# A new instruction order for a fused attention and token-MLP kernel, with vector work, row statistics and small loads moved between engines

## The chip, the cores and the metric

The kernel runs on one core of a Trainium2 chip. The metric is device time of one execution in microseconds (us), on the slowest core, which here is the only one. A profiled span, from the first to the last instruction, is about 1.8 us shorter than the time of the same run. Times of whole runs and spans of traces are therefore never mixed below: where stages are added up, the sum is a span.

The engines are PE (matmul), DVE (vector), ACT (activation functions), POOL (a second, general engine for elementwise work) and SP (which mostly issues DMAs). In the profile, PEld is PE's loading of weights, and a q after an engine's name is its instruction queue. Each executes its own list of instructions in order.

## The reference

Two branches share the input x (2048 tokens x 448) and are mixed by a gate per token. Cut to what matters:

```python
g = sigmoid((x * gate_w).sum(-1, keepdims=True))
# A: attention in 4 segments of 512 tokens, 16 heads of 28, plus a linear memory
phi = lambda t: where(t > 0, t + 1.0, exp(t))
for s in range(4):
    p = softmax(qs @ ks.T * scale + mask);  a_dot = p @ vs
    pq = phi(qs);  a_mem = (pq @ M) / (pq @ z + 1e-6)
    outs.append(sigmoid(beta) * a_mem + (1 - sigmoid(beta)) * a_dot)
    pk = phi(ks);  M = M + pk.T @ vs;  z = z + pk.sum(tokens)
a = concat(outs) @ wo
# B: LayerNorm over features, then an MLP over TOKENS
h = (x - mean) / sqrt(var + 1e-5)
u = gelu(einsum('bsd,sf->bdf', h, w1) + b1)          # w1 2048 x 1792
b = (einsum('bdf,fs->bds', u, w2) + b2).transpose(0, 2, 1)
return g * a + (1 - g) * b
```

## The kernel before

The kernel is a list of 1020 small operations in one string, PLAN. An item `name.args@engine+slots` names an operation, the engine that does it (P = PE, A = ACT, D = DVE, G = POOL, S = SP) and its buffers. A scheduler walks the string once, appends each operation to its engine's list and works out the semaphore waits from what each reads and writes. So the order in the string is the order of each engine, and changing a letter moves work between engines without touching the data flow.

```python
PLAN = """
warm@P ldwk.0@A dve0@D id@G ldx.0@S ldx.1@S ldwq.0@A setup@G ldwk.1@S acttab@A ldwq.1@S ldsm@S xw.0@D bn.0@D trx.0.3@P
...
ek.1.2@A pqm.1.1@G1 bn.8@D ldr.1@S1 pqe.1.0@A0 u.0.0@P0 u.1.0@P3 bn.12@D sc.0.2@P lnc.2@G u.1.1@P pqe.1.1@A1 ev.6@D
...                                                                                     (77 more lines)
```

phi is written as min(max(t, 0) + 1, exp(t)): a clamp (`pkm`, `pqm`), an exponential on ACT (`pke`, `pqe`) and a minimum on DVE (`pkn`, `pqn`). Five of the 12 clamps are on DVE and seven on POOL.

```python
def pmax(eng, dst, Rd, T, RT, hp, s):                      # pkm, pqm: the clamp, 128 x 1024
    op(eng, lambda e: e.tensor_scalar(dst..., two(T, hp, s), 0.0, 1.0, op0=ALU.max, op1=ALU.add), ...)
def pmin(dst, Rd, i):                                      # pkn, pqn
    op("DVE", lambda e: e.tensor_tensor(dst, dst, et[:, i, :], op=ALU.min), ...)
```

The LN has statistics on DVE (`bn`), a combination per four tiles on POOL (`lnc`), and an apply per tile (`lna`), eight on DVE and eight on POOL:

```python
def bn(eng, u, t):
    op("DVE", lambda e: e.bn_stats(st6[:, t, :], xtile(t)[:, 0, :]), ...)
    op("DVE", lambda e: e.bn_aggr(mv[:, t, :], st6[:, t, :]), ...)
def lnc(eng, u, g):     # 4 POOL operations on 128 x 4
    ... vpe = var + eps;  rstd = vpe ** -0.5;  vpe = -mean;  nmr = vpe * rstd
def lna(eng, u, t):
    op(eng, lambda e: e.tensor_scalar(x_t, x_t, rstd[:, t:t+1], nmr[:, t:t+1], op0=ALU.mult, op1=ALU.add), ...)
```

At the start DVE fills padded buffers with zeros, SP issues five small loads (gate weights, two biases, beta), and two copies of 128 x 128 (`xw`) widen the first x tiles. Part of the first PE transposes (`trx`) read what these copies write, and everything else on PE, apart from the warm-up matmuls (`NWARM` is their number), comes after the transposes:

```python
def dve0(eng, u):
    ...
    op("DVE", lambda e: e.memset(oAM[:], 0.0), writes=R_o)       # 128 x 3072 bf16
    op("DVE", lambda e: e.memset(wo_sb[:], 0.0), writes=[R_woz])
def xw(eng, u, h):
    op("DVE", lambda e: e.tensor_copy(x0[:, r, D:512], x0[:, r, 0:64]), reads=R_x[r], writes=R_xw[r])
def ldsm(eng, u): ...   # five dma_start by eng: gate_w (2), b1, b2, beta
```

The softmax here doesn't subtract the row's maximum and nothing guards it: scores larger than these inputs give would overflow.

## Time and profile before

| | before |
|---|---|
| time, median of 3 runs | 199.17 us (198.92 to 200.08) |
| span of the trace | 197.3 us |
| busy: PE / DVE / ACT / POOL | 176.7 / 143.8 / 118.5 / 84.4 us |
| share of the chain that ended last (the work followed back from the last instruction, at each step to what released it): PE / DVE / POOL | 38 / 25 / 23% |

The columns are length, then busy us of PE, PEld, DVE, ACT and POOL, the granted PE clock (1.00 is full), DMA share and GB/s.

```profile
31.00:35.00 4.00, 0.17 (x2) 0.10 (x2) 3.86 (x12) 0.70 (x2) 3.55 (x7) 1.00 1.32 208
35.40:38.80 3.40, 3.40 (x19) 1.00 (x19) 2.38 (x3) 1.88 (x1) 3.14 (x5) 0.50 0.78 160
100.20:103.60 3.40, 3.40 (x23) 1.08 (x24) 0.93 (x2) 3.33 (x3) 0.63 (x1) 0.50 0.16 40
```

The first is the 3.83 us wait of PE for the LN apply on POOL. The second comes right after it: PE is busy all of the time, but its clock is 0.50. The third, again 3.4 us at half clock, follows the second long wait (3.23 us, to 98.7). In this trace a long wait is paid for twice. And two groups of DVE in this trace (columns: line, engine, operation, output <- input, count, busy us, mean ns):

```profile
L618 DVE TENSOR_TENSOR t<-t 128x1024 bf16<-128x1024 bf16 x12 | 13.7, 1158 | 4.2 <-POOL t L609 4.1
L509 DVE COPY t<-t 128x128 bf16<-128x128 bf16 x2 | 0.3, 144 | 0.0
```

L618 is the minimum of phi. L509 are the two `xw` copies: 144 ns each, nobody would look at them.

### The profile page before, as it was taken

What the parts mean: (1) busy time and instruction counts of PE and PEld (TensorE: products, weight loads), DVE (VectorE), ACT (ScalarE), POOL (GpSimd) and SP (SyncE); (2) the same over time, 40 slices, a digit from 0 to 9 for tenths busy, and PEclk for the clock granted to TensorE, in tenths of its full rate; (3) what the DMA queues carried; (4) which work ended last, traced back from release to release, by engine and by line L of the source; (5) the groups of instructions that cost most, each with busy time, mean ns of one, the idle gap of its engine ahead of it and who ended that gap; (6) DMA issues with size and microseconds to landing.
All of it is one profiled execution on the core that took longest, in us unless ns stands there. A gap on an engine that the chain in (4) does not pass through costs nothing.

```text
span 197.3 us, 3599 instructions
## 1 busy us (share of the span) xinstructions
PE 176.7 (90%) x1464; PEld 79.9 (40%) x1471; DVE 143.8 (73%) x272; ACT 118.5 (60%) x108; POOL 84.4 (43%) x85
## 2 busy tenths in 40 slices
PE   7399993999599989989399997999999999999994
PEld 2243441234244434434235433444334444555554
DVE  5989999698718775479848938677999975397222
ACT  3338874349658956997366698598747787201100
POOL 2052299949922823779713239331523233220000
PEclk9999999699999999999969999999999999999999
DMA  6999999678587000218116064151073407166112
GB/s 163 208 233 268 240 208 236 136 185 219 137 182 205 12 0 3 53 27 221 23 26 186 5 186 145 44 151 35 31 205 106 127 27 216 53 200 190 56 33 71
DMA packets 50368, 24.92 MB, mean 126 GB/s; under 512 B 15088, under 2 KB 49968, under 8 KB 50352
## 3 DMA queue, kind: packets, MB, share of 16 engines
q1 hardware_dynamic: 49424, 24.24, 49.9%
q10 hardware_dynamic: 928, 0.46, 1.0%
q8 instruction: 11, 0.18, 0.4%
q14 instruction: 5, 0.04, 0.1%
HBM read 18.54 MB, written 1.84 MB: 103 GB/s over the span
## 4 chain that ended last, share of the span: by engine, by line
PE 38%; DVE 25%; POOL 23%; issue 6%; DMA 2%; SPq 2%; ACT 2%; another core or an unknown queue 0%; POOLq 0%; DVEq 0%
PE t L884 14%; POOL t L609 13%; PE t L831 10%; PE t L857 4%; POOL t L718 4%; PE t L736 3%; DVE t L367 3%; DVE t L618 3%; DVE t L791 3%; DMA t<-in_A_beta_dram 2%; PE t L695 2%; PE t L571 2%; POOL t L819 2%; DVE t L870 2%; SPq L357 2%
## 5 line engine op out<-in xcount | busy, mean ns | idle before, releaser
L705 ACT ACTIVATE t<-t 128x2048 bf16<-128x2048 f32 x40 | 75.1, 1877 | 30.8 <-PE t L695 28.2
L718 POOL TENSOR_SCALAR_AFFINE_SELECT t<-t 128x1024 bf16<-128x1024 bf16 (+1 forms) x40 | 38.0, 951 | 65.4 <-ACT t L705 61.0
L831 PE MATMUL t<-t 128*128 128x448 bf16 x224 | 49.8, 361 | 3.9 <-POOL t L819 3.8
L884 PE MATMUL t<-t 128*128 128x448 bf16 (+1 forms) x238 | 45.9, 342 | 0.1
L831 PEld LDWEIGHTS t<-t 128*128 128x128 bf16 x224 | 19.9, 99 | 27.5 <-issue 7.4
L884 PEld LDWEIGHTS t<-t 128*128 128x128 bf16 x238 | 22.6, 98 | 20.2 <-issue 2.3
L546 PE MATMUL t<-t 64*128 64x512 bf16 x224 | 27.5, 388 | 0.7 <-DVE t L469 0.3
L609 POOL TENSOR_SCALAR t<-t 128x1024 bf16<-128x1024 bf16 x7 | 26.5, 3795 | 1.6 <-DVE t L367 1.1
L365 ACT ACTIVATE t<-t 128x512 bf16<-128x512 f32 (+3 forms) x27 | 15.7, 599 | 12.8 <-PE t L546 6.0
L893 DVE SCALAR_TENSOR_TENSOR t<-t 128x448 bf16<-128x448 f32 (+1 forms) x17 | 10.7, 636 | 14.6 <-PE t L884 14.6
L367 DVE CAST t<-t 128x512 bf16<-128x512 f32 (+1 forms) x23 | 15.0, 654 | 8.0 <-PE t L546 6.1
L618 DVE TENSOR_TENSOR t<-t 128x1024 bf16<-128x1024 bf16 x12 | 13.7, 1158 | 4.2 <-POOL t L609 4.1
L546 PEld LDWEIGHTS t<-t 64*128 64x128 bf16 x224 | 10.4, 96 | 15.5 <-issue 3.1
L695 PE MATMUL t<-t 28*128 28x512 bf16 (+3 forms) x256 | 16.1, 304 | 0.1
L756 DVE STREAM_TRANSPOSE t<-t 128x512 f32<-128x512 f32 x16 | 11.2, 707 | 5.8 <-PE t L736 5.6
L571 PE MATMUL t<-t 64*128 64x449 bf16 x112 | 12.0, 350 | 2.8 <-DVE t L367 2.1
L857 PE MATMUL t<-t 128*128 128x448 bf16 x64 | 13.8, 354 | 0.0
L736 PE MATMUL t<-t 128*32 128x512 bf16 (+3 forms) x256 | 12.0, 312 | 1.4 <-POOL t L718 1.1
L842 DVE TENSOR_SCALAR t<-t 128x448 bf16<-128x448 f32 x10 | 6.7, 673 | 8.9 <-PE t L831 8.9
L614 ACT ACTIVATE t<-t 128x1024 bf16<-128x1024 bf16 x12 | 12.3, 1060 | 0.0
L777 DVE SCALAR_TENSOR_TENSOR t<-t 128x448 bf16<-128x448 f32 x16 | 11.9, 753 | 0.3
L796 DVE STREAM_TRANSPOSE t<-t 128x512 bf16<-128x512 bf16 x16 | 11.0, 697 | 0.1
(70 smaller groups left out, 151.9 us busy)
## 6 DMA issues: line engine op xcount, KB each, us to landing
t<-in_B_w_dram SPq DMA_DIRECT2D x7, 1024.0 KB, 6.3
t<-in_B_w_dram SPq DMA_DIRECT2D x8, 896.0 KB, 5.2
out_dram<-t SPq DMA_DIRECT2D x15, 112.0 KB, 1.7
t<-in_A_x_dram SPq DMA_DIRECT2D x3, 448.0 KB, 4.3
t<-t SPq DMA_DIRECT2D x6, 192.0 KB, 3.4
t<-in_A_wv_dram SPq DMA_DIRECT2D x2, 392.0 KB, 5.4
t<-in_A_x_dram SPq DMA_DIRECT2D x2, 224.0 KB, 3.6
t<-in_A_wo_dram SPq DMA_DIRECT2D x4, 98.0 KB
```

The source lines that it names most:

```text
L367: op(eng, lambda e: e.tensor_copy(out, in_), reads=reads, writes=writes)
L546: last = e.matmul(bank(bb)[:, 0:512], wkq[half[h], c, 128 * hg : 128 * hg + 128], xTb[half[h], b, i, :], start=(i == 0), stop=(i == 6), sk ...
L571: last = e.matmul(bank(bs[h])[:, 0 : D + 1], xTb[half[h], b, i, k0 : k0 + 128], wvx[half[h], (LC, UC)[h][i], 0 : D + 1], start=(i == 0), s ...
L609: op(eng, lambda e: e.tensor_scalar(dst.rearrange("p (g t) -> p g t", g=2), two(T, hp, s), 0.0, 1.0, op0=ALU.max, op1=ALU.add), reads=[RT[ ...
L618: op("DVE", lambda e: e.tensor_tensor(dst, dst, et[:, i, :], op=ALU.min), reads=[Rd, R_et[i]], writes=[Rd])
L695: last = e.matmul(bank(hl)[:, c0 : c0 + w], kT[r, hg, s * 512 + j * 128 : s * 512 + j * 128 + 128], qT[r, hg, s * 512 + 128 * j : s * 512 ...
L705: op("ACT", lambda e: e.activation(punit(i).rearrange("p (a q) -> p a q", a=4), ps[:, 0:4, :], ACT.Exp, scale=SCALE), reads=R_bank[0:4], w ...
L718: op("POOL", lambda e: e.affine_select(d, d, pattern=pat, compare_op=ALU.is_ge, fill=0.0, base=0, channel_multiplier=-1), reads=[R_P[i]], ...
L736: last = e.matmul(bank(b)[32 * hl : 32 * hl + 32, 128 * j : 512], vaug[:, 4 * s + j, 32 * h : 32 * h + 32], p4[:, hl, c0 : c0 + w], start= ...
L831: op("PE", lambda e: e.matmul(bank(b)[:, 0:D], w[:, st, (ft % 2) * 128 : (ft % 2) * 128 + 128], xtile(st)[:, 0, :], start=(st == 0), stop= ...
L857: last = e.matmul(bank(b)[:, 0:D], oT[:, hg, T * 128 : T * 128 + 128], wo_sb[:, hg, :], start=(hg == 0), stop=(hg == NHG - 1), skip_group_ ...
L884: op("PE", lambda e, b=b, f=f, c0=c0, n=n: e.matmul(bank(b)[:, 0:n], w[:, f, c : c + 128], uT[:, f, c0 : c0 + n], start=(f == 0), stop=(f ...
```

## The change

The intent is to take slow work off POOL, to give the row statistics to POOL instead, to free SP of small issues, and to plan the order anew with measured durations. The same 1020 operations are kept. By engine, 7 clamps, 8 LN applies and 6 products of the memory part go from POOL to DVE; some output scalings and copies go from DVE to ACT. The core of the diff, cut:

```diff
-NWARM = 8
+NWARM = 7
 PLAN = """            # all 79 lines differ; the start and one clamp, as an example
-warm@P ldwk.0@A dve0@D id@G ldx.0@S ldx.1@S ldwq.0@A setup@G ldwk.1@S acttab@A ldwq.1@S ldsm@S xw.0@D bn.0@D trx.0.3@P
+warm@P ldwk.0@A dve0@D id@G ldx.0@S ldx.1@S ldwq.0@A ldsm@G ldwk.1@S acttab@A ldwq.1@S ldwv.0@S trx.0.2@P xw.0@D
-... pqm.1.1@G1 ...
+... pqm.1.1@D1 ...
 def dve0(eng, u):
-    op("DVE", lambda e: e.memset(oAM[:], 0.0), writes=R_o)
 def setup(eng, u):
+    op("POOL", lambda e: e.memset(oAM[:], 0.0), writes=R_o)
 def bn(eng, u, t):
-    op("DVE", lambda e: e.bn_aggr(mv[:, t, :], st6[:, t, :]), ...)
 def lnc(eng, u, g):
-    ...                       # 4 POOL operations from mean and variance
+    tt2(d, me, mo, ALU.subtract, True)      # me, se, mo, so: halves' means and sums in st6
+    tt2(d, d, d, ALU.mult)
+    tt2(w, se, so, ALU.add, True)
+    ts2(w, w, 1.0 / D, 1e-5, ALU.add)
+    ts2(d, d, 0.25, 0.0, ALU.add)
+    tt2(d, d, w, ALU.add)
+    ... rstd = d ** -0.5; tt2(sd, me, mo, ALU.add); ts2(sd, sd, -0.5, ...); nmr = sd * rstd    # 10 in all
```

Line numbers shift: the clamp is L609 before and L608 after, the minimum L618 and L617, the LN apply L819 and L833, the `xw` copy L509 and L508.

## The prediction

> **What bounds the kernel now.** I read the page first, then the chain of work that ended last, the costliest groups, the table of 10 us windows, and the timelines of the engines where these pointed.
>
> ```profile
> span 197.3 us, 3599 instructions
> PE 176.7 (90%) x1464; PEld 79.9 (40%) x1471; DVE 143.8 (73%) x272; ACT 118.5 (60%) x108; POOL 84.4 (43%) x85
> ...
> PE 38%; DVE 25%; POOL 23%; issue 6%; DMA 2%; SPq 2%; ACT 2%; another core or an unknown queue 0%; POOLq 0%; DVEq 0%
> ```
>
> PE is busiest by far, yet it is only 38% of the chain that ended last. POOL, busy 43%, is 23% of that chain: 45 us in which the end waited for POOL. So this is a PE-bound kernel that is held up.
>
> ```profile
> L609 POOL TENSOR_SCALAR t<-t 128x1024 bf16<-128x1024 bf16 x7 | 26.5, 3795 | 1.6 <-DVE t L367 1.1
> L609 DVE TENSOR_SCALAR t<-t 128x1024 bf16<-128x1024 bf16 x5 | 2.9, 588 | 0.0
> L819 POOL TENSOR_SCALAR t<-t 128x448 bf16<-128x448 bf16 x8 | 5.7, 714 | 0.2
> L819 DVE TENSOR_SCALAR t<-t 128x448 bf16<-128x448 bf16 x8 | 4.2, 564 | 0.0
> L811 POOL TENSOR_TENSOR t<-t 128x4 f32<-128x4 f32 x4 | 4.4, 1108 | 0.3
> ```
>
> These groups show whose work it is. L609 is the clamp of phi, max(t,0)+1: 3795 ns on POOL against 588 ns on DVE for the same shape. L819 applies the LN, L811 is its power -0.5. The chain in order of time shows it on the path:
>
> ```profile
> 28.02 4.04 POOL t L609
> ...
> 44.10 7.61 POOL t L609 x2
> 51.73 1.10 DVE t L618
> 52.83 0.61 DVE t L367
> 53.49 1.50 PE t L571 x14
> ```
>
> Two clamps on POOL, then the DVE minimum that needs them, then a PSUM copy queued behind that minimum, then PE. An in-order DVE carries POOL's delay to PE. The wait view has the other direct case:
>
> ```profile
> PE t L831 <- POOL t L819: 3.8, 1, 3.8
> PE t L749 <- DVE t L842: 3.2, 1, 3.2
> PE t L571 <- DVE t L367: 2.1, 1, 2.1
> ```
>
> The first is PE at 31 us waiting for the LN on POOL. The second is at 95 to 98.7 us, behind three clamps and two products on POOL. The windows say when the bound changes (columns: length, then busy us of PE, PEld, DVE, ACT, POOL, clock, DMA share, GB/s):
>
> ```profile
> 30.00:40.00 10.00, 6.17 (x35) 1.89 (x37) 8.20 (x17) 3.58 (x3) 9.20 (x14) 0.83 1.00 182
> 90.00:100.00 10.00, 6.77 (x64) 3.31 (x61) 8.77 (x15) 4.58 (x6) 7.22 (x6) 1.00 0.40 107
> 140.00:150.00 10.00, 9.11 (x76) 3.93 (x76) 9.86 (x18) 5.63 (x3) 3.22 (x4) 1.00 0.40 116
> 180.00:190.00 10.00, 10.00 (x54) 5.16 (x53) 2.84 (x4) 1.45 (x2) 0.00 (x0) 1.00 0.40 118
> ```
>
> Early, POOL and DVE starve PE; around 145 DVE is full; the end is pure PE. The change can win little in the last 40 us.
>
> **What the Trainium skill says.** (1) "GPSIMD Engine Reference", section "4.1 Engine selection", calls POOL about 2x slower for two-input elementwise work and one-input work "roughly line-rate". The trace disagrees for the clamp: 3795 / 588 = 6.5x. (2) "SBUF — State Buffer", section "Who interferes with whom": copy and tensor_scalar on DVE in a 2-port mode share a port pair with POOL, and the second to issue fully blocks. The trace agrees in direction: the DVE clamp took 0.42 us at 21.75, with POOL idle, and 1.25 us at 28.49, beside the POOL clamp of 4.06 us; not blocked to its end, though. The LN apply took 0.35 us alone and 0.95 us beside POOL. So clearing POOL also shortens DVE. (3) "DMA: Bandwidth & Descriptors", section "SWDGE vs HWDGE vs iDMA": a DMA issued by POOL has its descriptors made in software, exposed to that same port lock. No run so far has one. (4) "TensorE: Matmul & The Clock Gate", section "Back-to-back issue gap": N/2.4 + 2.5 ns, 189 ns for 448 columns. The last 80 matmuls (52 of 448 columns, 28 of 224) took 12.53 us, 190 ns per 448: PE there is at its rate (the same section's 131 ns for a sustained stream at 512 columns is not seen here).
>
> **The change part by part.** The two order lists hold the same 1020 operations; engines, banks and order differ.
>
> Clamps: 7 leave POOL, -26.5 us there, and cost DVE 7 x 0.42 = 2.9 us. LN applies: 8 leave POOL, -5.7, and cost DVE 8 x 0.45 = 3.6 (between 0.35 and 0.56). Six products of the memory part (L785, 1073 ns on POOL, 628 on DVE): -6.4 and +3.8. Statistics: 16 aggregates leave DVE, 16 x 0.182 = -2.9; POOL does 10 small operations per group instead of 4, six more at about 0.27 from start to start, 4 x 6 x 0.27 = +6.5. The zero fill of the product buffer, 1.34, goes from DVE to POOL. Four output scalings, one bias copy and one weight padding go from DVE to ACT (-2.6 - 0.6 - 0.9), one PSUM copy comes (+0.6). Sums: POOL 84.4 - 26.5 - 5.7 - 6.4 + 6.5 + 1.3 = 54; DVE 143.8 + 2.9 + 3.6 + 3.8 - 2.9 - 1.3 - 2.6 - 0.6 - 0.9 + 0.6 = 146, perhaps 3 to 5 lower for the port; ACT 118.5 + 4 x 0.72 + 0.6 + 0.9 - 0.5 = 122. PE loses one warm-up matmul, nothing else.
>
> What is on the path? I cut both lists at the first score block (L695) of each of the eight score groups, P0 to P7, and summed each engine's work in every stage with durations of the trace before (start-to-start, us): token MLP matmul 0.19, Q/K pair 1.52, V pair 1.37, score block 0.33, PV 0.66, output projection 0.76, state 0.95; DVE copies 0.6, min 0.8, clamp 0.4, transpose 0.63; exp 1.8; mask 0.95. The stage's floor is its busiest engine; what the stage took above that is waiting. Stage starts are the L695 starts of the PE timeline: 16.3, 44.15, 63.0, 80.5, 99.8, 121.4, 140.1, 155.7.
>
> ```
> stage  before: took  floor     excess | after: floor  my estimate
> start         16.3   DVE 14.8   1.5   |  DVE 12.9     14.5
> P0            27.8   DVE 23.6   4.2   |  DVE 22.6     25.0
> P1            18.8   PE 16.0    2.8   |  DVE 14.8     16.6
> P2            17.5   PE 16.0    1.5   |  PE 14.4      16.0
> P3            19.3   PE 15.0    4.3   |  PE 13.1      14.8
> P4            21.6   PE 19.4    2.2   |  PE 21.4      23.3
> P5            18.7   PE 16.9    1.8   |  PE 20.1      21.8
> P6            15.6   DVE 14.0   1.6   |  PE 13.8      15.3
> P7 to end     41.6   PE 38.0    3.6   |  PE 37.3      40.9
> sum          197.2       173.7 23.5   |      170.4    188.2
> ```
>
> The three stages with POOL on the chain (P0, P1, P3) have 11.3 us of excess; the others 1.5 to 2.2 each (P7's includes a 2.5 us tail of last copy and store). I gave the changed stages the excess of the quiet ones, 1.5 to 1.9, and P0 2.4, since DVE is nearly full there. That takes 5.4 off these three and 0.3 off the others; the rest comes from floors, 173.7 - 170.4 = 3.3, because the new order spreads PE and DVE more evenly. A run took about 1.8 more than the traced span (199.0 against 197.3), so this table gives 190.0. A plan with true durations should also wait less in the quiet stages. If excess there fell from 1.7 to about 1.2, eight times 0.5 takes 4 off: 186. I choose the middle, **188.0 us**, 0.944 of before.
>
> **The rivals.** (a) **DVE takes POOL's place.** DVE keeps 146 us and is the floor of the first three stages, 50 of 188 us; the minimum and the PSUM copies queue on one in-order engine. For it: 140:150 shows 9.86 of 10 busy and PE still waiting. Against it: its sum hardly grows, and P4 to P7 leave it 15.2, 15.0, 8.4, 23.7 against PE's 21.4, 20.1, 13.8, 37.3. It would make 193 to 196. (b) **Transfers hold the front.** DMA share is 0.92 to 1.09 in the first 40 us, and the last x tile landed at 28.05. For it: bytes do not change. Against it: no compute engine waited over 0.3 us for a large load, and taking five small issues off SP (3.27 to 5.40 us, 2.1 us) moves the large ones up. If it holds, P0 loses 3 us: 191. (c) **Small loads through POOL come late.** They gate a tanh that stands on ACT before the weight padding and the first copies, and the transposed biases before V. Before, they landed at 9.7, already a 1.9 us wait of PE. If software descriptors push them to 12, the start grows by 2 us: 190. (d) **Full success:** excess under 1 us everywhere, 182.
>
> **Range and chances.** Range 182 to 194: (d) below; (a) or (b) with (c) above. Within 2% would need over 195.2, almost nothing gained though 26 us of POOL leaves the chain; only a strong (a) does that. Faster by over 2%: 0.91; within 2%: 0.07; slower: 0.02.
>
> **What would show the steps right or wrong.** Right: POOL busy near 54 and under 10% of the chain; all L609-type clamps on DVE at 0.4 to 0.6 us; PE's share of the chain well over half; stages P0, P1, P3 at about 25, 17, 15; PE's waits for LN and for the copies behind the minimum gone; DVE 141 to 147. Wrong: DVE over 35% of the chain with PE waiting for PSUM copies (a); PE or DVE waits for loads of x or W1 in the first 40 us (b); ACT or PE idle until a beta landing at about 10 us or later (c); a quiet stage (P4, P5) that takes over 2.5 us above its floor, which would mean that the new order is worse than its sums.

## The result, and the profile after

The median of four runs is **190.77 us** (190.20 to 191.28); the kernel before had 199.62 us in the same rounds (198.92 to 200.81). The ratio is 0.955, with a 95% interval of 0.949 to 0.961. Ratios here are the mean time of one kernel's fast runs over that of the other's of the same rounds, so not quite the ratio of the medians. Predicted were 188.0 us, 2.8 us (1.5%) too few, and a range of 182 to 194. The head and the chain of the page after:

```profile
span 188.6 us, 3618 instructions
PE 175.7 (93%) x1470; PEld 81.9 (43%) x1470; DVE 140.2 (74%) x271; ACT 122.2 (65%) x110; POOL 57.8 (31%) x94
...
PE 66%; DVE 19%; POOL 4%; issue 3%; ACT 2%; DMA 2%; SPq 1%; DVEq 0%
```

PE did the same work in 8.7 us less. POOL's share of the chain fell from 23% to 4%, PE's rose from 38% to 66%. The costliest groups that answer to those shown of before:

```profile
L617 DVE TENSOR_TENSOR t<-t 128x1024 bf16<-128x1024 bf16 x12 | 9.7, 805 | 0.0
L833 DVE TENSOR_SCALAR t<-t 128x448 bf16<-128x448 bf16 x16 | 8.1, 534 | 1.3 <-POOL t L829 1.2
L608 DVE TENSOR_SCALAR t<-t 128x1024 bf16<-128x1024 bf16 x12 | 5.8, 483 | 2.2 <-DMA t<-t 1.3 <-ACT t L364 0.8
L508 DVE COPY t<-t 128x128 bf16<-128x128 bf16 x2 | 3.5, 2600 | 0.0
```

All 12 clamps are on DVE at 483 ns. The minimum, which nobody touched, fell from 1158 to 805 ns, and the sum of the two branches (128 x 512) from 705 to 443 ns. But the two little copies went from 144 to 2600 ns each (they overlap: together 3.5 us). The waits of PE that are left (columns: total us, times, longest us):

```profile
PE t L517 <- DVE t L508: 2.1, 1, 2.1
...
PE t L845 <- DVE t L833: 1.3, 1, 1.3
PE t L659 <- DVE t L759: 1.1, 1, 1.1
```

The waits of 3.8 and 3.2 us are gone. The longest single one left is at the start, for those copies. Cut at the first score block of each of the eight groups, as in the prediction:

```
stage     before   predicted   after   off    floor   above floor
start      16.3      14.5      20.9   +6.4    12.9       8.0
P0         27.8      25.0      22.0   -3.0    22.6      -0.6
P1         18.8      16.6      17.9   +1.3    14.8       3.1
P2         17.5      16.0      16.1   +0.1    14.4       1.7
P3         19.3      14.8      14.0   -0.8    13.1       0.9
P4         21.6      23.3      22.3   -1.0    21.4       0.9
P5         18.7      21.8      20.6   -1.2    20.1       0.5
P6         15.6      15.3      14.2   -1.1    13.8       0.4
P7 to end  41.6      40.9      40.7   -0.2    37.3       3.4
span      197.3     188.2     188.6
```

(The stages of before add up to 197.2 and those of after to 188.7, from rounding. The floor is the prediction's, with durations of the trace before; DVE's work in P0 took less than that, so P0 lies below it.) The total of this table is nearly exact, and that is luck: the start took 6.4 us more than predicted, the rest 6.0 less. (The 188.0 us took another 2 us off what this table gives, for a better plan.) So there is something in the start to find. The trace after there (columns: start us, duration us, engine, line, operation):

```profile
3.75 0.58 POOL L356 DMA_DIRECT2D t<-in_A_beta_dram  x1
...
4.12 3.49 DVE L508 COPY t<-t 128x128 bf16<-128x128 bf16 x2
...
4.84 2.68 POOL L443 MEMSET t<- 128x3072 bf16 x1
...
7.63 2.10 PE L517 MATMUL t<-t 128*128 128x128 bf16 x18 [2.08 <-DVE t L508]
...
11.00 4.62 PE L545 MATMUL t<-t 64*128 64x512 bf16 x28 [1.27 <-DVE t L366]
```

And the first Q/K pair of before:

```profile
9.85 1.69 PE L546 MATMUL t<-t 64*128 64x512 bf16 x14
```

The copies began at 4.12, in the middle of a row of POOL instructions (DMA issues from 1.45 to 4.33, fills from 4.33 to 7.52), and ended at 7.57 and 7.61, right after the last fill. PE waited 2.08 us and then ran slowly: 28 matmuls of the first pairs took 4.62 us, against 2 x 1.69 before.

### The profile page after: what moved, and what is told of

It is laid out like the page before. It is cut to its first block, busy times and chain, and to the rows that moved or that the text cites. A ratio compares the mean times of both kernels' runs of the same rounds, so it can differ in the third digit from the quotient of the medians.

```text
span 188.6 us, 3618 instructions
## 1 busy us (share of the span) xinstructions
PE 175.7 (93%) x1470; PEld 81.9 (43%) x1470; DVE 140.2 (74%) x271; ACT 122.2 (65%) x110; POOL 57.8 (31%) x94
## 4 chain that ended last, share of the span: by engine, by line
PE 66%; DVE 19%; POOL 4%; issue 3%; ACT 2%; DMA 2%; SPq 1%; DVEq 0%
PE t L898 21%; PE t L845 16%; PE t L545 8%; PE t L871 7%; PE t L694 4%; PE t L735 4%; PE t L570 4%; DVE t L366 3%; DMA t<-t 2%; DVE t L617 2%; DVE t L508 2%; DVE t L833 2%; POOL t L812 2%; DVE t L803 1%; DVE t L608 1%
## 5 line engine op out<-in xcount | busy, mean ns | idle before, releaser
L845 PE MATMUL t<-t 128*128 128x448 bf16 x224 | 48.7, 354 | 1.8 <-DVE t L833 1.3
L545 PE MATMUL t<-t 64*128 64x512 bf16 x224 | 28.0, 392 | 3.4 <-DVE t L366 2.6
L845 PEld LDWEIGHTS t<-t 128*128 128x128 bf16 x224 | 20.1, 98 | 24.4 <-issue 5.3
L364 ACT ACTIVATE t<-t 128x512 bf16<-128x512 f32 (+4 forms) x27 | 16.6, 636 | 12.6 <-PE t L517 5.0
L907 DVE SCALAR_TENSOR_TENSOR t<-t 128x448 bf16<-128x448 f32 (+1 forms) x17 | 11.0, 649 | 16.0 <-PE t L898 15.9
L871 PE MATMUL t<-t 128*128 128x448 bf16 x64 | 13.8, 353 | 0.0
L881 ACT ACTIVATE t<-t 128x448 bf16<-128x448 f32 x8 | 5.8, 722 | 11.8 <-DVE t L884 11.4
L755 DVE STREAM_TRANSPOSE t<-t 128x512 f32<-128x512 f32 x16 | 11.0, 700 | 1.2 <-PE t L735 1.2
L735 PE MATMUL t<-t 128*32 128x512 bf16 (+3 forms) x256 | 11.1, 301 | 0.7 <-DVE t L366 0.4
L776 DVE SCALAR_TENSOR_TENSOR t<-t 128x448 bf16<-128x448 f32 x16 | 11.4, 724 | 0.2
L759 DVE STREAM_TRANSPOSE t<-t 128x512 f32<-128x512 f32 x12 | 8.4, 697 | 4.3 <-PE t L748 4.3
L884 DVE TENSOR_SCALAR t<-t 128x448 bf16<-128x448 f32 x8 | 6.0, 744 | 6.8 <-PE t L871 6.7
```

The source lines that it names most:

```text
L364: op("ACT", lambda e: e.activation(out, in_, ACT.Copy), reads=reads, writes=writes)
L545: last = e.matmul(bank(bb)[:, 0:512], wkq[half[h], c, 128 * hg : 128 * hg + 128], xTb[half[h], b, i, :], start=(i == 0), stop=(i == 6), sk ...
L735: last = e.matmul(bank(b)[32 * hl : 32 * hl + 32, 128 * j : 512], vaug[:, 4 * s + j, 32 * h : 32 * h + 32], p4[:, hl, c0 : c0 + w], start= ...
L845: op("PE", lambda e: e.matmul(bank(b)[:, 0:D], w[:, st, (ft % 2) * 128 : (ft % 2) * 128 + 128], xtile(st)[:, 0, :], start=(st == 0), stop= ...
L871: last = e.matmul(bank(b)[:, 0:D], oT[:, hg, T * 128 : T * 128 + 128], wo_sb[:, hg, :], start=(hg == 0), stop=(hg == NHG - 1), skip_group_ ...
```

## The experiments

All twelve gave correct results; all profiled runs are fast ones. Names with b_ start from the kernel before, those with a_ from the kernel after.

A word on noise first. Of the 36 runs of the kernel before in the experiments' rounds, 15 are slow and left out (their clocks are 0.949 to 0.958); one run of a_best is, too. The 21 fast ones remain. Their spans lie on a ladder with the run's mean granted clock: 195.7 us at 0.991 (one run), 197.0 to 197.5 at 0.983 (eleven), 197.7 to 198.6 at 0.974 (five), 198.9 to 199.5 at 0.966 (three); one at 0.935 and 199.3 doesn't fit. One stretch of 3.4 us at half clock lowers the mean by 3.4 x 0.5 / 197.3 = 0.0086, which is the step of the ladder. (The length of 3.4 us comes from the traces: in before the clock is 0.83 over the 10 us from 30 to 40, and 0.17 x 10 / 0.5 = 3.4.) A straight line through the first 20 gives **1.1 us per stretch**, an estimate, for it is read from differences between runs. Carried on to 0.957 the line gives 200.4 us, and the slow runs at 0.957 and 0.958 have 200.4 to 201.2. So spans are compared below with their clocks beside them.

| kernel | order | clamps / LN / products on | median us | ratio to before (95%) | span | clock |
|---|---|---|---|---|---|---|
| before | old | mixed | 199.62 | | 197.3 | 0.983 |
| b_clamps_dve | old | DVE / mixed / mixed | 194.13 | 0.979 (0.972 to 0.986) | 192.1 | 0.972 |
| b_all_dve | old | DVE / DVE / DVE | 195.21 | 0.976 (0.969 to 0.983) | 193.7 | 0.974 |
| a_all_pool | new | mixed / mixed / mixed | 208.55 | 1.042 (1.034 to 1.049) | 206.3 | 0.950 |
| a_clamps_pool | new | mixed / DVE / DVE | 200.78 | 1.007 (1.001 to 1.013) | 199.0 | 0.974 |
| a_lna_pool | new | DVE / mixed / DVE | 193.37 | 0.969 (0.963 to 0.976) | 191.5 | 0.973 |
| after | new | DVE / DVE / DVE | 190.77 | 0.955 (0.949 to 0.961) | 188.6 | 1.000 |
| a_stats_old | new | as after | 190.84 | 0.961 (0.953 to 0.969) | 188.8 | 0.982 |
| a_fill_dve | new | as after | 188.22 | 0.941 (0.932 to 0.950) | 186.6 | 0.991 |
| a_xw_act | new | as after | 188.34 | 0.940 (0.934 to 0.947) | 186.7 | 1.000 |
| a_ldsm_sp | new | as after | 187.70 | 0.945 (0.936 to 0.955) | 184.9 | 1.000 |
| a_phk3 | new | as after | 189.67 | 0.957 (0.950 to 0.964) | 187.9 | 1.000 |
| a_best | new | as after | 186.12 | 0.932 (0.928 to 0.937) | 185.2 | 0.990 |
| a_best2 | new | as after | 186.47 | 0.937 (0.931 to 0.942) | 184.8 | 1.000 |

"Mixed" is the distribution of before, the same operations on the same engines as there.

### Order or engines?

Theory: the gain is POOL's work leaving the path, and the new order helps a little beyond that. Rival: the order does it, and the engines matter little. Two corners of the square are before and after; the other two have the order of one and the engines of the other.

**b_all_dve**: the old order, with the 21 operations on DVE.

```diff
-... pqm.1.1@G1 ... lna.2@G ... om.4@G ...        (7 clamps, 8 LN applies, 6 products)
+... pqm.1.1@D1 ... lna.2@D ... om.4@D ...
```

> The kernel before, in its old order, with all 21 elementwise operations that the change takes off POOL (7 clamps, 8 LN applies, 6 products) on DVE. Theory E (the engine of these operations is the gain, by the waits at 31 and 95 us and the half clock after each): PE's waits of 3.8 and 3.2 us go, both half-clock stretches of 3.4 us go, span 197.3 to about 188 us. Theory O (the new order is the gain; with the old one DVE, 95% busy in the first 40 us, takes POOL's place): span 194 to 197 us.

**a_all_pool**: the new order, with the same 21 operations back on POOL.

```diff
-... pqm.1.1@D1 ... lna.2@D ... om.4@D ...
+... pqm.1.1@G1 ... lna.2@G ... om.4@G ...
```

> The changed kernel, in its new order, with the same 21 operations back on POOL at the places that the new order gives them. Theory E: about 197 us or more, for the order was planned without these waits, perhaps over 200. Theory O: 189 to 192 us, the order keeps most of the gain.

The spans make a square. Old order: 197.3 with POOL, 193.7 without, a gain of 3.6. New order: 206.3 with POOL, 188.6 without, a gain of 17.7. Read the other way, the new order costs 9.0 us with the old engines and gains 5.1 with the new ones. Neither theory holds as stated: neither part alone gives the 8.7 us, and the two are 14.1 us more together than their separate effects (-3.6 and +9.0) add up to. The waits of PE in a_all_pool, and its chain, show why the order can't live with POOL:

```profile
PE t L845 <- POOL t L833: 6.7, 2, 3.7
PE t L845 <- DVE t L856: 4.8, 1, 4.8
```

```profile
PE 59%; POOL 18%; DVE 15%; ACT 3%; issue 3%; DVEq 0%
```

L845 is the token MLP, which the new order starts as soon as the LN should be ready; with eight applies on POOL it is not, and P0 takes 29.6 us and P1 23.2 (22.0 and 17.9 in after). Its clock of 0.950 is six stretches at half clock by the ladder's count (0.050 / (3.4 x 0.5 / 206.3) = 6.1), so, by an estimate, some 6 of the 17.7 us are what its long waits cost a second time.

The chain of b_all_dve:

```profile
PE 58%; DVE 33%; DMA 3%; issue 2%; SPq 2%; ACT 1%; another core or an unknown queue 0%; DVEq 0%
```

Here the prediction's rival (a) is seen alive: DVE has taken POOL's place, with 33% of the chain. P0 took 26.8 us, only 1.1 less than before. And Theory E's forecast for the two long waits failed. They are still there, with all 21 operations off POOL:

```profile
PE t L749 <- DVE t L842: 2.8, 1, 2.8
PE t L831 <- DVE t L819: 2.7, 2, 2.5
```

The second of the two long waits, which the prediction put down to clamps and products on POOL, was 3.2 us in before and is 2.8 here, where DVE works without a gap from 88.5 to 95.9 us ahead of it. So that wait belongs to the old order of DVE's work more than to POOL.

### Which operation?

**b_clamps_dve**: the old order, only the seven clamps on DVE.

```diff
-... pqm.1.1@G1 ... pkm.1.0@G1 ... pkm.1.1@G0 ... pqm.2.0@G2 ... pkm.2.1@G0 ... pqm.3.0@G0 ... pqm.3.1@G1
+... pqm.1.1@D1 ... pkm.1.0@D1 ... pkm.1.1@D0 ... pqm.2.0@D2 ... pkm.2.1@D0 ... pqm.3.0@D0 ... pqm.3.1@D1
```

> The kernel before, old order, with only its 7 POOL clamps moved to DVE; LN applies and products stay on POOL. All 21 operations moved gave a span of 193.7 us. Theory C (the clamps, 13.4% of the chain before, are what counts): span 193.5 to 195 us, nearly all of that. Rival N (the LN applies count as much, for the 3.8 us wait of PE at 31 us is theirs): span 195.5 to 197.5 us, and that wait stays above 3 us.

It took 5.2 us off the span (197.3 to 192.1), more than all 21 together. PE's wait for the LN fell from 3.8 to 1.7 us with the LN applies still on POOL, so more than half of it came from the clamps; the second long wait stayed at 3.2. The further 14 operations made the old order worse by 1.6 us (192.1 to 193.7, at nearly the same clock), and the stages place it in P0: 25.0 us with the clamps alone, 26.8 with all. DVE's busy time in P0 rose from 23.0 to 25.0 us there and passed PE's (23.3 and 23.6).

**a_clamps_pool** and **a_lna_pool**: the new order, with only the clamps, or only the eight LN applies, back on POOL.

```diff
-... pqm.1.1@D1 ... (7 clamps)                  # a_clamps_pool
+... pqm.1.1@G1 ...
-... lna.0@D ... lna.2@D ... (8 applies)        # a_lna_pool
+... lna.0@G ... lna.2@G ...
```

> The changed kernel with only its 7 former POOL clamps back on POOL; LN applies and products stay on DVE. All 21 back on POOL gave a span of 206.3 us, that is 17.7 us more. Theory C (the clamps carry it): 200 to 205 us, at least two thirds of the 17.7. Rival (LN and products carry it): under 197 us.

> The changed kernel with only the 8 former POOL LN applies back on POOL (0.71 us each). In the old order, moving LN and products to DVE on top of the clamps lost 1.6 us (192.1 to 193.7). Theory F (DVE is full in the first 40 us, so sharing the LN pays): span 187 to 188.2. Theory Q (POOL's 10 small operations per group come first in its queue, and the applies then come late): span 189.5 to 191.5.

The clamps on POOL cost 10.4 us (199.0 against 188.6) and eat the whole gain of the change; that is 59% of the 17.7, a little under the two thirds that were expected. The LN applies cost 2.9 (191.5), and PE waits 3.3 us for them, as Theory Q had it. A run of after at the clock of these two (0.973) had a span of 189.4, which makes it 9.6 and 2.1. So the clamps are the change's core, in both orders. They also decide what the untouched minimum costs. With the clamps back, its group reads as it did before:

```profile
L617 DVE TENSOR_TENSOR t<-t 128x1024 bf16<-128x1024 bf16 x12 | 13.9, 1158 | 6.8 <-POOL t L608 6.8
```

That is 1158 ns here and in before, with clamps on POOL (1049 in a_all_pool), and 805 (after) or 730 (b_clamps_dve) in the same orders with all clamps on DVE. So POOL's clamps cost the minimum 4.2 us of DVE time in the new order and 5.1 in the old one. The six products were never moved alone; from 206.3 - 188.6 = 17.7 and 10.4 + 2.9 = 13.3, 4.4 us remain for them and for what the parts do to each other. That stays open.

### What happened at the start?

Theory: the fill on POOL holds the SBUF port that the two DVE copies need, so that they can't finish. Rival: the small loads come late through POOL, and ACT, held by the wait for beta, delays the start (the prediction's rival c). One more part of the change acts at the start, one warm-up matmul less. It was not tested alone, but a_xw_act and a_ldsm_sp, whose first pairs take only 3.2 us for 28 matmuls, have it too.

**a_fill_dve** takes away POOL's fill; the copies stay where they are. **a_xw_act** takes the copies off DVE; the fill stays.

```diff
 def dve0(eng, u):                                        # a_fill_dve
+    op("DVE", lambda e: e.memset(oAM[:], 0.0), writes=R_o)
 def setup(eng, u):
-    op("POOL", lambda e: e.memset(oAM[:], 0.0), writes=R_o)
```

```diff
-... xw.0@D ... xw.1@D ...                                # a_xw_act
+... xw.0@A ... xw.1@A ...
-    op("DVE", lambda e: e.tensor_copy(x0[:, r, D:512], x0[:, r, 0:64]), reads=R_x[r], writes=R_xw[r])
+    copy(eng, x0[:, r, D:512], x0[:, r, 0:64], R_x[r], R_xw[r])
```

> The changed kernel with one line undone: the zero fill of the product buffer is on DVE again, the small loads stay on POOL. Theory L (POOL's run of descriptors and fills at 3.75 to 7.5 us holds the port that the two 128x128 copies on DVE need): these copies fall from 3.49 us together to under 1 us, PE's wait of 2.08 us for them goes, the PE stays busy through its warm-up and the first pair takes about 1.7 us instead of 3.0; the first score block moves from 20.9 to about 17.5 us and the span from 188.6 to about 185.5 us. Rival R (the front is set by the loads and the copies wait for x): the copies start no earlier than 5.8 us anyway, span 188 to 189 us.

> The changed kernel with only the two 128x128 copies moved from DVE to ACT; the fill and the small loads stay on POOL. [...] Theory L: the copies take about 0.3 us each on ACT, right after x lands at 3.6 and 5.8 us; PE's wait of 2.08 us goes, span about 185.5 us, as in the run with the fill on DVE. Rival R (loads): no change, 188 to 189 us.

Both gained about the same: spans of 186.6 and 186.7, 2.0 and 1.9 us less than after. The spans of 185.5 us that were expected did not come. In a_fill_dve the two copies took 0.23 us together, and in a_xw_act all 28 transposes ran on from 4.27 with no wait for a copy. Nothing about the loads was changed in either. The theory holds in that the fill and the copies are in each other's way; that the port is the way is argued, and no trace records it. In a_fill_dve the slow first pairs are still there, again 28 matmuls in 4.62 us, and here the trace has a record of the clock:

```profile
8.50:11.90 3.40, 2.88 (x14) 1.02 (x16) 2.25 (x9) 1.13 (x2) 0.00 (x0) 0.50 1.23 193
```

So the pairs of after, with the same 4.62 us, most likely ran at half clock too, although its trace shows a clock of 1.00 throughout. Why it shows none is open.

The rival is not dead. In a_xw_act, where no blocked copy hides it, ACT waits 2.85 us for beta (0.49 in after), and PE then waits 1.25 and 0.67 us for copies on ACT behind that. The third experiment takes both causes away at once: SP issues the small loads again, and POOL, free of DMA issues, does its fill early.

**a_ldsm_sp**

```diff
-... ldwq.0@A ldsm@G ldwk.1@S acttab@A ldwq.1@S ldwv.0@S ...
+... ldwq.0@A ldwk.1@S acttab@A ldwq.1@S ldsm@S ldwv.0@S ...
```

> The changed kernel with only the small loads undone: the five of them issued by SP again, behind the weights. The fill stays on POOL but begins near 1.4 us instead of 4.8, so it ends near 4.7 us. If the port is held by whatever POOL runs (theory L), the two 128x128 copies end by 6 us, PE's 2.08 us wait goes, and the small loads land about 1 us earlier (9.7 instead of 10.7 us), against 2 us later issues of the V weights and of x transposed: span 185.5 to 187. If issuing the small loads from SP delays the large ones enough (the change's intent), span 188 to 190.

The span is 184.9 us, 3.7 less than after. Its timeline:

```profile
1.80 2.66 POOL L443 MEMSET t<- 128x3072 bf16 x1
...
4.11 0.40 DVE L508 COPY t<-t 128x128 bf16<-128x128 bf16 x1
4.26 2.47 PE L517 MATMUL t<-t 128*128 128x128 bf16 x28
...
8.31 3.19 PE L545 MATMUL t<-t 64*128 64x512 bf16 x28 [1.58 <-DVE t L366]
```

The fill is over at 4.46, and the first copy, begun at 4.11, ends 0.05 us later: here a fill that only writes held up a small DVE copy until it ended, as in after (7.52 and 7.57). The first pairs took 3.19 us instead of 4.62. The start fell from 20.9 to 17.2, and all stages after it are the same as in after to 0.1 us. The three experiments together divide these 3.7 us. The start took 20.9 us in after and 18.9 in a_fill_dve, which frees the copies but keeps the slow pairs and the late beta: 2.0 us are the blocked copies. It took 18.4 in a_xw_act, with free copies, fast pairs (28 matmuls in 3.20 us) and beta still at 10.8: about 0.5 us are the half clock, for most of its 1.4 us is hidden behind the wait for beta. And it took 17.2 here, where beta landed at 9.6: 1.2 us are the late beta. (In a_xw_act P2 took 16.6 us instead of 16.1, which is why its span shows only 1.9 of its 2.5.)

So moving five small loads to POOL, meant to help the large loads, was a loss on this kernel.

### The rest above the floor: P1 and P2

**a_stats_old** undoes the new row statistics: `bn_aggr` on DVE and four operations on POOL, as before. In P1, after's DVE waits 1.19 us for the combination `lnc.3` on POOL (ten operations, 40.41 to 44.0), and PE 1.28 us behind it.

```diff
 def bn(eng, u, t):
+    op("DVE", lambda e: e.bn_aggr(mv[:, t, :], st6[:, t, :]), ...)
 def lnc(eng, u, g):
-    ...       # ten POOL operations
+    ...       # the four of before
```

> The changed kernel with only the row statistics undone: 16 aggregates back on DVE, 4 instead of 10 small operations per group on POOL. It gives DVE 2.9 us more in the first 40 us, where it is 98% busy, and shortens each POOL chain by about 1.6 us. Theory D (DVE's time decides there, as the change assumes): span 1 to 2.5 us longer, 189.6 to 191. Theory P (the length of POOL's chain decides: the last group ran from 40.4 to 44.0 us, with DVE waiting 1.2 us and PE 1.3 us for it): span 0.5 to 1.5 us shorter, 187 to 188.

P1 fell from 17.9 to 15.9 us, and P0 rose from 22.0 to 23.2, the start from 20.9 to 21.4 and P2 from 16.1 to 16.6. (DVE is 99% busy from 20 to 40 us in after; over the whole of the first 40 it is 86%, not 98.) The sum is neutral, between the two theories: a span of 188.8 against 188.6, medians of 190.84 and 190.77. The move saves DVE 2.9 us where it is full (P0) and pays it back by a longer chain of POOL where DVE waits for it (P1). No gain of that part by itself shows.

**a_phk3** goes for P2, where a clamp waits for a transposing DMA (landed at 63.71) that still reads its buffer. A third buffer takes the wait away; the warm-up's buffer had to be laid over another one to make room.

```diff
-    phk = sb([128, 2, 1024])
+    phk = sb([128, 3, 1024])
-    dummy = sb([128, 640])
+    dummy = outst[:, 0:2, :].rearrange("p a d -> p (a d)")[:, 0:640]
-... pkm.2.0@D1 ... pkm.2.1@D0 ...
+... pkm.2.0@D2 ... pkm.2.1@D1 ...
```

> The changed kernel with a third buffer for the clamped keys (and the zeros of the warm-up put into a buffer that is used later, to make room). In the changed kernel DVE waits 1.34 us at 63.8 us until a transposing DMA has read such a buffer, and PE waits 1.08 us at 65.9 us behind it. Theory B (that wait ends last in its stage): it goes, and the span falls by about 1 us, to 187.6. Rival: DVE has other work in its queue just after, the time moves by under 0.3 us.

DVE's timeline in after, then in a_phk3:

```profile
61.79 0.68 DVE L676 TENSOR_TENSOR t<-t 128x512 bf16<-128x512 f32 x1
63.81 0.43 DVE L608 TENSOR_SCALAR t<-t 128x1024 bf16<-128x1024 bf16 x1 [1.34 <-DMA t<-t]
```

```profile
61.83 0.68 DVE L676 TENSOR_TENSOR t<-t 128x512 bf16<-128x512 f32 x1
62.43 0.41 DVE L608 TENSOR_SCALAR t<-t 128x1024 bf16<-128x1024 bf16 x1
```

The wait of 1.34 us is gone, and P2 took 15.3 us instead of 16.1. The span is 187.9, 0.7 less: about half of the wait reached the end.

### A version that beats both

**a_best** joins a_ldsm_sp and a_phk3, and moves the tanh of beta behind the second weight padding on ACT, so that ACT should not wait for beta.

```diff
-... ldwq.0@A ldsm@G ldwk.1@S acttab@A ldwq.1@S ldwv.0@S ...        (and phk, dummy, pkm as in a_phk3)
+... ldwq.0@A ldwk.1@S acttab@A ldwq.1@S ldsm@S ldwv.0@S ...
-... ex.2@D tb@A bn.1@D pair.0.1@P01 pad.1@A
+... ex.2@D bn.1@D pair.0.1@P01 pad.1@A tb@A
```

> The changed kernel with three repairs at once: small loads on SP again (span 184.9 alone), the third buffer for clamped keys (0.7 us alone), and the tanh of beta moved on ACT behind the padding of the weights, so that ACT no longer waits 1.89 us for beta with the padding behind it. If the three are at different places of one chain they add: 184.9 - 0.7 - about 1 (the padding comes 1.9 us earlier, and PE waited 0.4 + 0.7 us behind ACT) = 183.2 us, 0.927 of before. If the third is hidden by the loads of V and x: 184.2.

The median of six runs, one of them slow, is **186.12 us**, 0.932 of before, and it beats both kernels (five of its runs took 185.60 to 186.91 us, those of after 190.20 to 191.28, in other rounds). The start stayed at 17.2 us, though: moving the tanh only handed the wait from ACT to DVE, which uses its result before the first K copy (PE then waited 1.26 us for that copy). P2 is 15.3, as in a_phk3. In the profiled run P1 took 18.9 us, 1.0 more than in a_ldsm_sp, and the windows say why:

```profile
41.60:45.00 3.40, 1.74 (x17) 0.67 (x21) 3.40 (x8) 1.85 (x3) 1.08 (x2) 1.00 0.94 252
45.00:48.40 3.40, 3.40 (x28) 1.30 (x23) 3.33 (x6) 2.40 (x2) 1.10 (x1) 0.50 0.82 198
```

PE was busy for 1.74 of 3.40 us, with waits of 1.29 and 0.36 and nothing longer; the next 3.4 us ran at half clock. a_ldsm_sp has waits of the same lengths and no such stretch. So the lengths of the waits alone don't decide it; what does is open. Runs of a_best at a clock of 1.000 had spans of 183.8 to 184.4 us, the expectation's second case.

**a_best2** also puts DVE's use of beta behind the K copy in the list.

```diff
-bn.3@D bet@D pair.0.0@P23 eq.0.1@A btr@P1 ek.0.1@D eq.0.0@A ...      (otherwise a_best)
+bn.3@D pair.0.0@P23 eq.0.1@A btr@P1 ek.0.1@D bet@D eq.0.0@A ...
```

> The repaired kernel of the run before (185.2 us in its profile, 184.2 to 184.4 us in its timed runs without a half-clock stretch) with one more move: the small DVE operations on beta go behind the first copy of K instead of ahead of it. In the repaired kernel they ran from 9.87 to 12.03 us, the copy came at 12.03 us, and PE waited 1.26 us for it. If that wait was only handed from ACT to DVE, as the trace says, the third pair now starts near 12.1 instead of 12.8 us and the span is 183.6 us. If the third pair then waits for ACT's copies (they end near 12.6 us), nothing moves: 184.3 us.

A miss: 186.47 us, no faster than a_best, with a start of 17.3 us. The block of beta on DVE (10.93 to 13.09) is now in front of the next copies, and PE waits 0.77 us for it and 0.82 for a transposed tile. Each of these waits had another close behind, and P0 took 22.6 us, 0.6 more than in a_best.

## Why the prediction was right, point by point

**The bound** was read rightly in the main. PE was held up by POOL through DVE's order; with POOL at 4% of the chain and PE at 66%, PE works nearly through. One reading was wrong: the wait at 95 to 98.7 us was not POOL's, for it stays at 2.8 us with all 21 operations off POOL (b_all_dve). That the clamps carried it is shown by the experiment that puts only them back, which loses the whole gain. The signs that the prediction named came: POOL under 10% of the chain, clamps at 0.48 us, both long waits gone; DVE at 140.2 us is just under its 141 to 147.

**The sums**: ACT came to 122.2 us (122 predicted). POOL came to 57.8, not 54: its five DMA issues count as busy, 1.30 + 1.03 + 0.58 = 2.9 us, and the fill took 2.68 instead of the 1.34 of DVE. DVE came to 140.2; the sum was 146, "perhaps 3 to 5 lower for the port". That term was too small: the minimum alone gave 12 x (1158 - 805) ns = 4.2 us and the sum of the branches 12 x (705 - 443) ns = 3.1. Part of it was lost again by the 3.2 us of the slow copies. The minimum's share is shown to come from POOL's clamps (above). The other isn't: that sum takes 738 ns in b_clamps_dve and 482 in a_clamps_pool, so not the clamps account for it. Most of it is the order: from the old to the new one it falls from 705 to 600 ns with the products divided (before, a_all_pool), and from 643 to 443 with all of them on DVE (b_all_dve, after). That the shared port is how POOL slows DVE fits all of these, but no run shows the port itself.

**The stages**: the step that failed is the start, "my estimate" of 14.5 us, which took 20.9. Three terms are missing in it, 3.7 us in all. The first is the blocked copies: the prediction quoted the Trainium skill ("SBUF — State Buffer", section "Who interferes with whom", and "DMA: Bandwidth & Descriptors", section "SWDGE vs HWDGE vs iDMA") and took POOL's DMA issues to be the ones in danger. The victim was the other side: two DVE copies behind POOL's fill, 2.0 us by a_fill_dve. The second is the late beta, 1.2 us: the prediction had it as rival (c), worth 2 us, and left it out of the estimate. The third is the clock, about 0.5 us here. The Trainium skill, "TensorE: Matmul & The Clock Gate", section "Why this matters for your kernels", says to leave no PE-idle gaps of more than about 3 us, as one window of idle halves the clock. The trace of before agrees with that, and the prediction showed a clock of 0.83 in its own window of 30 to 40 us, but never costed it. The other 2.7 us over the estimate (17.2 in a_ldsm_sp against 14.5) stay unexplained; there and in before, which took 16.3, beta at 9.6 to 9.7 us still holds up ACT or PE for 1.9 us.

**The quiet stages**: P3 to P6 took 0.4 to 0.9 us above their floors, where the table of estimates gave them 1.5 to 1.9. The 4 us that the prediction thought a better plan might save there came (0.8 + 1.0 + 1.2 + 1.1 = 4.1 in P3 to P6), P0 gave 3.0 more, and together they paid for the start. P0's share fits DVE's shorter operations (21.4 us busy against the floor of 22.6), which is argued, not tested. The one stage after the start that was under-estimated is P1, by 1.3 us: DVE's wait of 1.19 us there for the longer POOL chain (a_stats_old) was not in the estimate. Half-clock stretches belong in this account: before had two in its trace and after none in mid-kernel, by the ladder 2 x 1.1 = 2.2 us of the 8.7, an estimate.

**The rivals**: (a), DVE takes POOL's place, didn't come in after (19% of the chain), but it is what happens with the old order and the new engines (33%), so the order is what defused it. (b), transfers, didn't come: PE and DVE wait for no large load. (c), late small loads, came in kind: beta landed at 10.7 us, and ACT waited. In after most of that wait is hidden behind the blocked copies; its share of the start is the 1.2 us above. (d), full success, was 182; a_best's best runs come to 185.6.

**What failed in the reading of the change** is that its two halves were added up as if each stood alone. The stage table was made of the new list and the new engines together, so its total could come near, with errors that happened to cancel; but the prediction's reason for the lower floors is the order alone, and with the old engines that order is a loss of 9.0 us. That the old order's wait for POOL came from planning with durations too short for it, as the change's intent suggests, is argued and not shown.

## What to carry to other kernels

An order list and its engine choice are one decision: test the moved operations and the new order in all four combinations before you credit either, as here the engines alone gave 3.6 us of 8.7 and the order alone lost 9.0. When a second engine is busy beside a vector engine in a kernel's first microseconds, look at the duration of the smallest operations there (144 ns before, 2600 after), not at the sums, because one of them may hold up everything. Count a wait of PE of over 3 us at its length plus about 1 us, the estimate from this kernel's runs, and read the mean clock of each run beside its time.

## What the Trainium skill lacked or had wrong

- "GPSIMD Engine Reference", section "4.1 Engine selection", calls one-input work "roughly line-rate" on POOL. The clamp took 3795 ns there and 588 ns (before) or 483 ns (after) on DVE; the LN apply, also of one input, took 714 and 564 ns.
- "SBUF — State Buffer", section "Who interferes with whom", has the second to issue blocked for the whole instruction. A DVE clamp beside POOL's clamp of 4.06 us took 1.25 us, so it was not blocked to its end. A 128 x 128 copy, on the other hand, lasted from 4.12 to 7.57 us over four POOL instructions in a row (after): it didn't finish between them. The page doesn't tell of a row of instructions, nor does this rule say whether a fill, which only writes, is enough; here it was (ends at 4.46 and 4.51 us in a_ldsm_sp).
- "TensorE: Matmul & The Clock Gate", section "Why this matters for your kernels", gives idle gaps of about 3 us as the danger, and no busy share. Half clock also followed a window of 3.4 us with PE busy for 1.74 us and no wait over 1.29 (a_best), and didn't follow the same waits in a_ldsm_sp.
- "DMA: Bandwidth & Descriptors", section "SWDGE vs HWDGE vs iDMA", says why small loads through POOL are slower to set up, but gives no time for it: here their issues occupied POOL for 0.58 to 1.30 us per load or pair (2.9 us for five), and beta landed 1.1 us later than through SP (10.7 against 9.6).
